# Window attention with a Sinkhorn mixture of experts: the products of two Strassen groups in one interleaved order, and the first unit's weight work placed later

## The chip, the cores and the metric

The kernel runs on one core of one Trainium2 chip. The metric is the device time of one execution in microseconds (us); before the change it is 1629.33 us, the median of three runs (1628.76 to 1629.43). The engines are TensorE (PE; its weight loads are listed apart as PEld), VectorE (DVE), ScalarE (ACT), GpSimd (POOL) and SyncE (SP), whose queue issues the DMAs. Each engine takes its instructions in the order in which they were written.

## The reference, cut to what matters

Attention in a window of 64 positions, then a soft mixture of eight experts, whose weights come from a Sinkhorn iteration. Everything is float32. The experts' two matrix products take most of the time:

```python
def _moe_ref(x, w_gate, w1, w2):          # x: 2304 x 512, w1: 8 x 512 x 1024, w2: 8 x 1024 x 512
    logits = x @ w_gate
    logits = logits - logits.max()
    P = np.exp(logits)
    for _ in range(8):
        P /= P.sum(1, keepdims=True) + 1e-09
        P /= P.sum(0, keepdims=True) + 1e-09
        P *= N / E
    for e in range(E):
        h = np.maximum(x @ w1[e], 0.0)
        ye = h @ w2[e]
        out += P[:, e:e + 1] * ye
```

## The kernel before

A first phase (up to about 207 us) computes the attention and part of the first expert for all rows. The second phase is what the change touches. It goes over the rows in three passes of six tiles of 128 rows; the inputs x of a pass lie in SBUF as sums and differences (`xc`, seven of them). Each expert's 1024 hidden columns are taken 256 at a time; one such piece is a **group** (90 in all), and two groups make a **unit** (45 units, 15 in each pass).

**A group's first product** is done with Strassen's scheme in Winograd's form: seven products of 2 x 2 blocks, numbered 1 to 7, instead of eight. Each product is six matmuls of 384 columns (`product`, line 175): the float32 operands are split into a high and a low part in fp32r, and high x high, high x low and low x high are added. Products add up in three PSUM banks: 1 and 2 in bank a (profile name `qa`), 6, 7 and 4 in b (`qb`), 5 and 3 in c (`qc`). Each bank exists twice and a group takes one of each, so two groups can be open at once. Between the products other engines read the banks:

- ScalarE copies bank a after product 1 to `p1` (line 195; the profile calls it `p`).
- VectorE (`add`, line 188) adds bank b after product 6 to `p1`, giving `u2`; bank b after product 7 to `p1`, giving `u3`; bank c after product 5 to `u3`; bank b after product 4 to `p1`; bank c after product 3 to `u2`. The profile calls `u2` and `u3` both `u`.
- ScalarE (`relu`, line 180) makes the high part of the four quarters of the hidden activations `g`, from bank a after product 2, from `u3`, from `p1` and from `u2`. VectorE (`low`, line 185) makes the low parts of the same four. The first of the four reads a PSUM bank and an SBUF tile, the other three read two SBUF tiles.

A product may write a bank again only when what was read from it before has been read: product 2 waits for the copy, products 7 and 4 for the adds of bank b, and product 3 for the add that reads bank c after product 5.

**A unit** is: the seven products of its even group, the seven of its odd group, then 72 matmuls of 512 columns (`mm2`, line 235), which multiply the activations of both groups by `w2` and whose sums VectorE adds to the output tiles (`acc`).

**The weights of later groups** are prepared along the way. `fetch1` and `fetch2` issue the loads of w1 and w2 of a group into a ring of three buffers (`stg`) on the SyncE queue; a load waits until the buffer's last content has been used. `sums1` forms four sums of w1's blocks on GpSimd (lines 126 to 129). `split1` and `split2` make high parts on ScalarE (lines 143, 155) and low parts on GpSimd (lines 146, 156). In unit u with groups s and s+1, the code before calls: during the even group `split2(s+2)` and `fetch1(s+3)`, during the odd group `sums1(s+2)`, `split2(s+3)` and `fetch2(s+4)`, after the products `split1(s+2)`, `sums1(s+3)` and `fetch2(s+5)`, and after the third tile of `mm2` `split1(s+3)` and `fetch1(s+4)`. Ahead of the first unit stand, in this order, `fetch2(1)`, `split1(1)`, `split2(0)`, `split2(1)`, `fetch2(2)`, `fetch2(3)`, `fetch1(2)`; behind them comes the start of the Sinkhorn iteration, whose exponential is on ScalarE (line 674).

The order of everything is the order of the code: no scheduler moves an instruction.

Of the kernel before, what the change touches and what calls it, by code (L numbers as in the profile page):

```python
# [21 lines left out]
def window_attention_sinkhorn_moe(ctx: ExitStack, tc: tile.TileContext, q, k, v, w_gate, w1, w2, out):  # L22
    nc = tc.nc
# [51 lines left out]
    class Ring:  # L75
# [5 lines left out]
        def open(self, pool):  # L81
            if self.nb:
                self.pool_b, self.n, self.i = pool, self.na + self.nb, self.na
# [21 lines left out]
    def fetch1(i):  # L105
        if i < len(groups):
            _, e, c = groups[i]
            stg = r_stg.new()
            nc.sync.dma_start(out=stg, in_=w1[e, :, c * 2 * P:(c + 1) * 2 * P].rearrange("(k p) f -> p k f", p=P))
            raw1[i] = stg  # L110

    def fetch2(i):
        if i < len(groups):
            _, e, c = groups[i]
            stg = r_stg.new().rearrange("p k f -> p (k f)").rearrange("p (c d) -> p c d", c=2)
            nc.sync.dma_start(out=stg, in_=w2[e, c * 2 * P:(c + 1) * 2 * P, :].rearrange("(c p) d -> p c d", p=P))
            raw2[i] = stg
# [31 lines left out]
    def split2(i):  # L149
        if i >= len(groups):  # L150
            return
        src = raw2.pop(i)
        for j in range(2):
            w = r_w2.new()
            nc.scalar.copy(out=w[:, 0], in_=src[:, j])  # L155
            nc.gpsimd.tensor_tensor(out=w[:, 1], in0=src[:, j], in1=f32(w[:, 0]), op=ALU.subtract)  # L156
            wt2[i, j] = w
# [4 lines left out]
    ps = {}  # L162
    gt_ = {}

    class Group:
# [21 lines left out]
        def add(self, dst, bank, src):  # L187
            nc.vector.tensor_tensor(out=dst, in0=bank, in1=src, op=ALU.add)  # L188

        def run(self, extra):  # L190

            a, b, c = ps["a"](), ps["b"](), ps["c"]()
            p1, u2, u3 = r_p.new(), r_u2.new(), r_u3.new()
            self.product(1, a, True)
            nc.scalar.copy(out=p1, in_=a)  # L195
            extra(0)
            self.product(6, b, True)
            self.add(u2, b, p1)
            self.product(2, a, False)
            self.relu(0, 0, a)  # L200
            extra(1)
            self.product(7, b, False)
            self.add(u3, b, p1)
            self.low(0, 0, a)
            self.product(5, c, True)
            self.add(u3, c, u3)
            self.relu(1, 1, u3)
            self.product(4, b, False)
            self.add(p1, b, p1)
            self.relu(1, 0, p1)  # L210
            self.low(1, 1, u3)
            extra(2)
            self.product(3, c, False)
            self.add(u2, c, u2)
            self.relu(0, 1, u2)
            self.low(1, 0, p1)
            self.low(0, 1, u2)
            extra(3)
            wt1.pop(self.i)


    side = {}
# [64 lines left out]
    with tc.manual_schedule():  # L287
# [348 lines left out]
        with ExitStack() as p2:  # L636
            ring_b = p2.enter_context(tc.tile_pool(name="ring_b", bufs=1, reuse_waits="tile"))
            sk_p = p2.enter_context(tc.tile_pool(name="sk", bufs=2, reuse_waits="tile"))
            ps_m = p2.enter_context(tc.tile_pool(name="ps_m", bufs=2, space=PSUM, reuse_waits="tile"))
            for nm in "abc":  # L640
                ps[nm] = lambda nm=nm: ps_m.tile([P, 512], F32, tag=f"q{nm}", name=f"q{nm}")[:, :NB]
            ps["y"] = lambda: ps_m.tile([P, 512], F32, tag="y", name="yp2")
            for r in rings.values():
                r.open(ring_b)

            def side_tile():
                return ring_b.tile([P, 4 * 2 * NB], F32, tag="side", name="side")

            side["acc"] = side_tile().rearrange("p (t d) -> p t d", t=TP)
            fetch2(1)  # L650
            split1(1)
            split2(0)
            split2(1)
            fetch2(2)
            fetch2(3)
            fetch1(2)


            pending = []
            state = {}  # L660

            def sk_tile(shape, name):
                n = 1
                for x in shape[1:]:
                    n *= x
                t = ps["c"]()[:shape[0], :n]
                return t.rearrange("p (t e) -> p t e", e=shape[2]) if len(shape) == 3 else t

            def sk_exp():
                mp = sk_tile([P, 1], "mb")  # L670
                nc.tensor.matmul(mp, lhsT=ones[0:1, :], rhs=max2, start=True, stop=True)
                nm = sk_p.tile([P, 1], F32, tag="nm", name="nm2", bufs=1)
                nc.vector.tensor_copy(out=nm, in_=mp)
                nc.scalar.activation(out=pv, in_=logit, func=AF.Exp, bias=nm)

            def sk_row():
                r = sk_p.tile([P, T], F32, tag="r", name="r")
                nc.vector.tensor_reduce(out=r, in_=prob[:, 0:T, :], axis=AX.X, op=ALU.add)
                nc.vector.reciprocal(out=r, in_=r)
                nc.vector.tensor_tensor(out=pv, in0=pv, in1=r[:, :, None].to_broadcast([P, T, E]), op=ALU.mult)  # L680

            def sk_col():
                cp = sk_tile([P, T + 1, E + 1], "cp")
                nc.tensor.matmul(cp, lhsT=part, rhs=prob, start=True, stop=True)
                c = sk_p.tile([P, E], F32, tag="c", name="c")
                nc.vector.tensor_reduce(out=c, in_=cp[:, :, 0:E].rearrange("p t e -> p e t"), axis=AX.X, op=ALU.add)
                nc.vector.reciprocal(out=c, in_=c)
                nc.vector.tensor_tensor(out=pv, in0=pv, in1=c[:, None, :].to_broadcast([P, T, E]), op=ALU.mult)

            sk_exp()  # L690
            sk_row()
            pending += [lambda: (sk_col(), sk_row())] * (ITERS - 1) + [sk_col]

            def step():
                if pending:
                    pending.pop(0)()


            def next_sums(p, j):
                if j == 0:  # L700
                    side["xt"] = side_tile().rearrange("p (i k n) -> p i k n", i=4, k=2)
                x = ring_b.tile([P, KD, 2 * P], F32, tag="xr2", name="xr2")
                nc.sync.dma_start(out=x, in_=xd_f[p - 1][j])
                x_sums(side["xt"][:, :, :, j * P:(j + 1) * P], x, nc.gpsimd)

            def next_slot(p, slot):
                if slot < 3:
                    nc.sync.dma_start(out=f32(xc[slot]), in_=xd_r[p - 1][:, slot])
                else:
                    nc.scalar.copy(out=xc[slot][:, 0], in_=side["xt"][:, slot - 3])  # L710

            def next_low(slot):
                nc.vector.tensor_tensor(out=xc[slot][:, 1], in0=side["xt"][:, slot - 3], in1=f32(xc[slot][:, 0]), op=ALU.subtract)

            n_units = len(groups) // 2
            per = n_units // NPASS
            for u in range(n_units):
                pas, at = divmod(u, per)
                more = pas + 1 < NPASS
                s = 2 * u  # L720

                edge = more and at == per - 1

                def even(k):
                    if k == 1:
                        split2(s + 2)
                        fetch1(s + 3)
                    elif k == 3 and more and per - 5 <= at < per - 5 + TP // 2:
                        next_sums(pas + 1, at - (per - 5))

                def odd(k):
                    if k == 0:
                        sums1(s + 2)
                    elif k == 1:
                        split2(s + 3)
                        fetch2(s + 4)
                    if edge and k in (0, 1, 3):
                        next_slot(pas + 1, (0, 1, None, 2)[k])

                Group(s).run(even)  # L740
                Group(s + 1).run(odd)
                order = (4, 5, 3, 6)
                if edge:
                    for slot in order:
                        next_slot(pas + 1, slot)
                split1(s + 2)
                sums1(s + 3)
                fetch2(s + 5)
                for t in range(TP):
                    mm2(u, t)  # L750
                    if t % 2 == 0:
                        step()
                    if t == 2:
                        split1(s + 3)
                        fetch1(s + 4)
                    if edge and t < 4:
                        next_low(order[t])
# [28 lines left out]
```

## Time and profile before

| | us |
|---|---|
| median of three runs | 1629.33 |
| the profiled execution | 1628.85 |
| its span, first to last instruction | 1626.8 |
| TensorE busy in it | 1608.7 |
| GpSimd busy | 1010.4 |
| VectorE busy | 828.4 |
| ScalarE busy | 623.1 |

The rows come from one profiled execution. Times in a timeline are microseconds from the start of its span. A timeline row gives start, length, engine, line, operation, output and inputs; "x6" is six instructions in one row, whose length goes from the first one's start to the last one's end. Matmuls are pipelined, so that rows of neighbouring products overlap by some 0.16 us; where a product's turn begins is read from the starts. In brackets stands how long the engine was idle ahead of the row and which instruction ended that.

### The profile page before, as it was taken

How to read it: one execution, taken by the hardware profiler on the slowest of the kernel's cores; microseconds unless marked ns; L12 is line 12 of the kernel's file. 1: busy time of each engine (PE TensorE's matmuls, PEld its weight loads, DVE VectorE, ACT ScalarE, POOL GpSimd, SP SyncE). 2: the span in 40 equal slices, each digit the busy share in tenths (PEclk: the TensorE clock that was granted, in tenths of full speed). 3: DMA queues.
4: the chain of work that ended last, by engine and by line, in shares of the span. 5: the costliest groups of instructions: out<-in, count | busy, mean ns of one | idle time of the engine just before them, and what ended most of it. 6: DMA issues, size and time to landing. Idle time of an engine off the chain costs nothing.

```text
span 1626.8 us, 23899 instructions
## 1 busy us (share of the span) xinstructions
PE 1608.7 (99%) x9253; PEld 1432.6 (88%) x9253; DVE 828.4 (51%) x1411; ACT 623.1 (38%) x1267; POOL 1010.4 (62%) x942
## 2 busy tenths in 40 slices
PE   8999989999999999999999999999999999999999
PEld 6888879988988998998898899899889889989988
DVE  6666455664544454554454445445545445544543
ACT  5666533342342333334333233333433323423331
POOL 5244475676666668676666656876756666675670
PEclk9999999999999999999999999999999999999999
DMA  9876531222222222432122212222622222221211
GB/s 216 195 166 147 152 117 52 65 78 65 65 66 77 65 91 78 152 114 78 65 65 71 73 54 77 91 78 85 194 65 65 78 65 64 66 75 56 67 50 39
DMA packets 156624, 145.86 MB, mean 90 GB/s; under 512 B 62112, under 2 KB 123040, under 8 KB 156512
## 3 DMA queue, kind: packets, MB, share of 16 engines
q1 hardware_dynamic: 156512, 144.35, 30.2%
q8 instruction: 72, 1.18, 0.3%
q14 instruction: 40, 0.33, 0.1%
HBM read 121.65 MB, written 15.73 MB: 84 GB/s over the span
## 4 chain that ended last, share of the span: by engine, by line
PE 96%; DVE 1%; DMA 1%; ACT 1%; issue 0%; SPq 0%; POOL 0%; ACTq 0%; POOLq 0%; DVEq 0%
PE yp L235 45%; PE qb L175 17%; PE qa L175 12%; PE qc L175 12%; PE yp L519 3%; PE hp L505 3%; PE vp L425 1%; PE sp L375 1%; PE tp L410 1%; PE tp L347 1%; DMA q<-in_q_dram 1%; ACT s L394 0%; DMA stg<-in_moe_w_dram 0%; DVE nm L382 0%; DVE s L379 0%
## 5 line engine op out<-in xcount | busy, mean ns | idle before, releaser
L235 PE MATMUL yp<-w2c,g 128*128 128x512 f32 x3240 | 746.6, 390 | 0.0
L235 PEld LDWEIGHTS yp<-w2c,g 128*128 128x128 f32 x3240 | 607.0, 188 | 125.0 <-DVE acc L255 0.9
L156 POOL TENSOR_TENSOR w2c<-stg,w2c 128x512 fp32r<-128x512 f32 x180 | 229.1, 1295 | 326.3 <-PE qb L175 315.1
L255 DVE SCALAR_TENSOR_TENSOR acc<-yp,prob,acc 128x512 f32<-128x512 f32 x240 | 180.2, 751 | 412.6 <-PE yp L235 405.7
L175 PE MATMUL qb<-xc,w1c 128*128 128x384 f32 x1620 | 328.6, 337 | 0.0
L175 PEld LDWEIGHTS qb<-xc,w1c 128*128 128x128 f32 x1620 | 284.1, 188 | 4.0 <-DVE u L188 0.6
L146 POOL TENSOR_TENSOR w1c<-stg,w1c 128x512 fp32r<-128x512 f32 (+1 forms) x180 | 179.7, 1020 | 103.8 <-ACT w1c L143 103.8
L175 PE MATMUL qa<-xc,w1c 128*128 128x384 f32 x1080 | 223.0, 341 | 5.5 <-ACT p L195 5.0
L146 POOL TENSOR_TENSOR w1c<-ws,w1c 128x1024 fp32r<-128x1024 f32 x90 | 218.4, 2426 | 0.0
L175 PE MATMUL qc<-xc,w1c 128*128 128x384 f32 x1080 | 216.4, 335 | 0.0
L175 PEld LDWEIGHTS qa<-xc,w1c 128*128 128x128 f32 x1080 | 189.7, 189 | 19.0 <-ACT p L195 15.0
L188 DVE TENSOR_TENSOR u<-qb,p 128x384 f32<-128x384 f32 x180 | 99.9, 555 | 199.0 <-PE qb L175 198.8
L143 ACT CAST w1c<-ws 128x1024 fp32r<-128x1024 f32 x90 | 94.7, 1052 | 252.7 <-POOL ws L129 252.7
L175 PEld LDWEIGHTS qc<-xc,w1c 128*128 128x128 f32 x1080 | 190.5, 188 | 0.0
L180 ACT ACTIVATE g<-u 128x384 fp32r<-128x384 f32 x180 | 94.7, 526 | 173.9 <-DVE u L188 172.2
L195 ACT COPY p<-qa 128x384 f32<-128x384 f32 x90 | 42.6, 473 | 272.6 <-PE qa L175 272.6
L185 DVE SCALAR_TENSOR_TENSOR g<-u,g 128x384 fp32r<-128x384 f32 x180 | 139.6, 775 | 8.0
L155 ACT CAST w2c<-stg 128x512 fp32r<-128x512 f32 x180 | 101.9, 617 | 8.6 <-DMA stg<-in_moe_w_dram 8.6
L188 DVE TENSOR_TENSOR u<-qc,u 128x384 f32<-128x384 f32 x180 | 99.9, 555 | 2.6
L180 ACT ACTIVATE g<-qa 128x384 fp32r<-128x384 f32 x90 | 44.2, 491 | 135.6 <-PE qa L175 135.6
L404 POOL TENSOR_TENSOR s<-s,rr 128x512 f32<-128x512 f32 x36 | 37.5, 1040 | 78.1 <-DVE rr L403 41.2
L143 ACT CAST w1c<-stg 128x512 fp32r<-128x512 f32 (+1 forms) x180 | 82.4, 506 | 5.0 <-DMA stg<-in_moe_w_dram 5.0
(124 smaller groups left out, 1324.4 us busy)
## 6 DMA issues: line engine op xcount, KB each, us to landing
stg<-in_moe_w_dram SPq DMA_DIRECT2D x182, 512.0 KB, 3.5
xd_r<-xs SPq DMA_DIRECT2D x36, 128.0 KB, 2.6
xc<-xd_r SPq DMA_DIRECT2D x6, 768.0 KB, 5.8
out_dram<-acc SPq DMA_DIRECT2D x18, 256.0 KB, 3.1
vs<-v SPq DMA_DIRECT2D x35, 128.0 KB, 4.1
k<-in_k_dram SPq DMA_DIRECT2D x16, 256.0 KB, 4.7
q<-in_q_dram SPq DMA_DIRECT2D x16, 256.0 KB, 5.2
v<-in_v_dram SPq DMA_DIRECT2D x16, 256.0 KB, 4.1
```

The costliest lines, as they stand in the source:

```text
L143: nc.scalar.copy(out=w[:, 0, sl].rearrange("p s k f -> p (s k) f"), in_=src)
L146: nc.gpsimd.tensor_tensor(out=o, in0=src, in1=f32(h), op=ALU.subtract)
L155: nc.scalar.copy(out=w[:, 0], in_=src[:, j])
L156: nc.gpsimd.tensor_tensor(out=w[:, 1], in0=src[:, j], in1=f32(w[:, 0]), op=ALU.subtract)
L175: nc.tensor.matmul(bank, lhsT=w[:, a, ws, kk, :], rhs=xc[xs][:, b, kk, :], start=(first and j == 0), stop=(j == 5), skip_group_check=not f ...
L180: nc.scalar.activation(out=g[:, 0, :], in_=src, func=AF.Relu)
L185: nc.vector.scalar_tensor_tensor(out=g[:, 1, :], in0=src, scalar=0.0, in1=f32(g[:, 0, :]), op0=ALU.max, op1=ALU.subtract)
L188: nc.vector.tensor_tensor(out=dst, in0=bank, in1=src, op=ALU.add)
L235: nc.tensor.matmul(yp, lhsT=g[:, a, o:o + P], rhs=w[:, x, :], start=(i == 0), stop=(i == 11))
L255: nc.vector.scalar_tensor_tensor(out=at, in0=yp, scalar=pr, in1=at, op0=ALU.mult, op1=ALU.add)
L505: nc.tensor.matmul(hp, lhsT=w1s[c][:, a, kk, :], rhs=xs[j][:, b, kk, :], start=(i == 0), stop=(i == 3 * KD - 1))
L519: nc.tensor.matmul(yp, lhsT=g[:, a, o * P:(o + 1) * P], rhs=w[:, x, :], start=(i == 0), stop=(i == 11))
```

## The change

The method `run` of a group becomes nine short methods, and a unit calls those of its two groups (g, the even one, and h, the odd one) in an order written out. The seven products of a group stay as they are. Their order in a unit was g1 g6 g2 g7 g5 g4 g3, then the same of h; it becomes g1 g6 g5 g2 g7 h1 g4 h6 g3 h2 h7 h5 h4 h3. The reads of the banks on VectorE and ScalarE go with the products, except that g's read of c for `u3` follows h's copy, and that g's last low part (`end`) follows h7. `split2(s+2)` moves to just ahead of g2, `sums1(s+2)` to behind h1, and `split2(s+3)` to behind h2.

The second part concerns the first unit alone. `split2(1)` and `fetch1(2)` move from ahead of it to behind h2, and `split2(2)`, `fetch1(3)`, `sums1(2)`, `split2(3)` and `fetch2(4)` from its products to behind them.

```diff
-        def run(self, extra):
...
+        def open(self):
+            self.p1, self.u2, self.u3 = r_p.new(), r_u2.new(), r_u3.new()
+            self.a = ps["a"]()
+            self.product(1, self.a, True)
+            nc.scalar.copy(out=self.p1, in_=self.a)
+
+        def b6(self):
+            self.b = ps["b"]()
+            self.product(6, self.b, True)
+            self.add(self.u2, self.b, self.p1)
+
+        def a2(self):
+            self.product(2, self.a, False)
+            self.relu(0, 0, self.a)
+
+        def b7(self):
+            self.product(7, self.b, False)
+            self.add(self.u3, self.b, self.p1)
+
+        def c5(self):
+            self.c = ps["c"]()
+            self.product(5, self.c, True)
+
+        def c22(self):
+            self.low(0, 0, self.a)
+            self.add(self.u3, self.c, self.u3)
+            self.relu(1, 1, self.u3)
+
+        def b4(self):
+            self.product(4, self.b, False)
+            self.add(self.p1, self.b, self.p1)
+            self.relu(1, 0, self.p1)
+            self.low(1, 1, self.u3)
+
+        def c3(self):
+            self.product(3, self.c, False)
+            self.add(self.u2, self.c, self.u2)
+            self.relu(0, 1, self.u2)
+            self.low(1, 0, self.p1)
             wt1.pop(self.i)
+
+        def end(self):
+            self.low(0, 1, self.u2)
...
             split2(0)
-            split2(1)
             fetch2(2)
             fetch2(3)
-            fetch1(2)
...
                 def even(k):
+                    if u == 0:
+                        return
...
                 def odd(k):
-                    if k == 0:
+                    if u == 0:
+                        if k == 1:
+                            split2(1)
+                            fetch1(2)
+                    elif k == 0:
                         sums1(s + 2)
...
-                Group(s).run(even)
-                Group(s + 1).run(odd)
+                g, h = Group(s), Group(s + 1)
+                g.open()
+                even(0)
+                g.b6()
+                g.c5()
+                even(1)
+                g.a2()
+                g.b7()
+                h.open()
+                odd(0)
+                g.c22()
+                g.b4()
+                even(2)
+                h.b6()
+                g.c3()
+                h.a2()
+                odd(1)
+                even(3)
+                h.b7()
+                g.end()
+                h.c5()
+                h.c22()
+                h.b4()
+                odd(2)
+                h.c3()
+                h.end()
+                odd(3)
...
-                split1(s + 2)
+                if u == 0:
+                    split2(2)
+                    fetch1(3)
+                    sums1(2)
+                    split1(2)
+                    split2(3)
+                    fetch2(4)
+                else:
+                    split1(s + 2)
                 sums1(s + 3)
                 fetch2(s + 5)
```

What that makes of the order of the instructions is shown at three places. The rows are those of unit 21, whose timeline is among the rows below; the other units after the first have the same. A number behind a name tells instances apart, and `w1c_0`, `p1_0`, `u2_0`, `u3_0` belong to g, `w1c_1`, `p1_1`, `u2_1`, `u3_1` to h; `xc0` to `xc6` are the seven inputs, one for each product (0 for product 1, 1 for 2, 2 for 3, 6 for 4, 3 for 5, 4 for 6, 5 for 7).

TensorE, the seven products of h in the unit before:

```order
L175 MATMUL qa_8858<-xc0_81,w1c_1_8733 128x384 x6
L175 MATMUL qb_8859<-xc4_85,w1c_1_8733 128x384 x6
L175 MATMUL qa_8858<-xc1_82,w1c_1_8733 128x384 x6
L175 MATMUL qb_8859<-xc5_86,w1c_1_8733 128x384 x6
L175 MATMUL qc_8860<-xc3_84,w1c_1_8733 128x384 x6
L175 MATMUL qb_8859<-xc6_87,w1c_1_8733 128x384 x6
L175 MATMUL qc_8860<-xc2_83,w1c_1_8733 128x384 x6
```

TensorE, the same unit after, from g's third product on:

```order
L175 MATMUL qc_8803<-xc3_84,w1c_0_8677 128x384 x6
L175 MATMUL qa_8787<-xc1_82,w1c_0_8677 128x384 x6
L175 MATMUL qb_8795<-xc5_86,w1c_0_8677 128x384 x6
L175 MATMUL qa_8836<-xc0_81,w1c_1_8733 128x384 x6
L175 MATMUL qb_8795<-xc6_87,w1c_0_8677 128x384 x6
L175 MATMUL qb_8863<-xc4_85,w1c_1_8733 128x384 x6
L175 MATMUL qc_8803<-xc2_83,w1c_0_8677 128x384 x6
L175 MATMUL qa_8836<-xc1_82,w1c_1_8733 128x384 x6
L175 MATMUL qb_8863<-xc5_86,w1c_1_8733 128x384 x6
L175 MATMUL qc_8905<-xc3_84,w1c_1_8733 128x384 x6
L175 MATMUL qb_8863<-xc6_87,w1c_1_8733 128x384 x6
L175 MATMUL qc_8905<-xc2_83,w1c_1_8733 128x384 x6
```

Three products stand between h's products on `xc0` and `xc1` (1 and 2), where there was one; between the last two on `qc` stands one product, as before.

VectorE at the end of g and the start of h's tail, before:

```order
L185 SCALAR_TENSOR_TENSOR g0_5_8844<-p1_0_8787,g0_5_8844 128x384
L185 SCALAR_TENSOR_TENSOR g1_1_8854<-u2_0_8788,g1_1_8854 128x384
L188 TENSOR_TENSOR u2_1_8862<-qb_8859,p1_1_8861 128x384
L188 TENSOR_TENSOR u3_1_8863<-qb_8859,p1_1_8861 128x384
L185 SCALAR_TENSOR_TENSOR g0_0_8889<-qa_8858,g0_0_8889 128x384
L188 TENSOR_TENSOR u3_1_8863<-qc_8860,u3_1_8863 128x384
L188 TENSOR_TENSOR p1_1_8861<-qb_8859,p1_1_8861 128x384
```

VectorE after, in the stretch in which h's products 7, 5 and 4 are read:

```order
L185 SCALAR_TENSOR_TENSOR g0_5_8860<-p1_0_8784,g0_5_8860 128x384
L188 TENSOR_TENSOR u3_1_8835<-qb_8863,p1_1_8833 128x384
L185 SCALAR_TENSOR_TENSOR g1_1_8878<-u2_0_8785,g1_1_8878 128x384
L185 SCALAR_TENSOR_TENSOR g0_0_8887<-qa_8836,g0_0_8887 128x384
L188 TENSOR_TENSOR u3_1_8835<-qc_8905,u3_1_8835 128x384
L188 TENSOR_TENSOR p1_1_8833<-qb_8863,p1_1_8833 128x384
```

The low part of g's `u2` now stands between h's adds of `qb` and of `qc` for `u3`, ahead of the low part from `qa`.

ScalarE at the start of the first unit, before (the first two rows are the casts of `split2(1)`):

```order
L155 CAST w2c_6_3167<-stg_2_3152 128x512
L155 CAST w2c_7_3170<-stg_2_3152 128x512
L674 ACTIVATE prob_74<-logit_73,nm2_3181 128x18x8
L195 COPY p1_0_3191<-qa_3188 128x384
L180 ACTIVATE g0_4_3214<-qa_3188 128x384
L155 CAST w2c_0_3216<-stg_0_3173 128x512
L155 CAST w2c_1_3219<-stg_0_3173 128x512
```

ScalarE after:

```order
L685 ACTIVATE prob_74<-logit_73,nm2_3173 128x18x8
L194 COPY p1_0_3180<-qa_3183 128x384
L180 ACTIVATE g0_4_3212<-qa_3183 128x384
L194 COPY p1_1_3221<-qa_3224 128x384
L180 ACTIVATE g1_0_3234<-u3_0_3182 128x384
L180 ACTIVATE g0_5_3243<-p1_0_3180 128x384
L180 ACTIVATE g1_1_3261<-u2_0_3181 128x384
L180 ACTIVATE g0_0_3270<-qa_3224 128x384
L155 CAST w2c_6_3272<-stg_2_3152 128x512
L155 CAST w2c_7_3275<-stg_2_3152 128x512
```

The exponential and g's copy no longer have casts ahead of them; the casts of `split2(1)` stand behind h's first Relu.

## Rows read from the trace of the kernel before

**Rows 1.** The page: the span, the busy time of TensorE, and of its costliest groups the weight loads for bank c (line, engine, operation, output and inputs, count, busy us, mean ns of one, then idle us ahead of them).

```profile
span 1626.8 us, 23899 instructions
PE 1608.7 (99%) x9253; PEld 1432.6 (88%) x9253; DVE 828.4 (51%) x1411; ACT 623.1 (38%) x1267; POOL 1010.4 (62%) x942
...
L175 PEld LDWEIGHTS qc<-xc,w1c 128*128 128x128 f32 x1080 | 190.5, 188 | 0.0
```

**Rows 2.** The waits of TensorE's weight loads from 246 us to the end: who waited for whom, us in total, times, longest.

```profile
PEld qa L175 <- ACT p L195: 9.6, 36, 0.3
...
PEld qb L175 <- DVE u L188: 0.3, 1, 0.3
```

**Rows 3.** The timeline of TensorE's matmuls in unit 21 (873.76 to 905.02 us): product 5 and 3 of g, product 2 of h.

```profile
877.98 1.20 PE L175 MATMUL qc<-xc,w1c 128*128 128x384 f32 x6
...
880.06 1.20 PE L175 MATMUL qc<-xc,w1c 128*128 128x384 f32 x6
...
883.29 1.31 PE L175 MATMUL qa<-xc,w1c 128*128 128x384 f32 x6
```

**Rows 4.** The timeline of the weight loads in the same unit: of product 3 of g, 6 and 2 of h, and 3 of h.

```profile
879.88 1.05 PEld L175 LDWEIGHTS qc<-xc,w1c 128*128 128x128 f32 x6
...
881.97 1.05 PEld L175 LDWEIGHTS qb<-xc,w1c 128*128 128x128 f32 x6
883.29 0.99 PEld L175 LDWEIGHTS qa<-xc,w1c 128*128 128x128 f32 x6 [0.27 <-ACT p L195]
...
887.45 1.05 PEld L175 LDWEIGHTS qc<-xc,w1c 128*128 128x128 f32 x6
```

**Rows 5.** The timelines of ScalarE, VectorE and GpSimd in the same unit.

```profile
877.10 0.49 ACT L180 ACTIVATE g<-qa 128x384 fp32r<-128x384 f32 x1 [1.55 <-PE qa L175]
...
882.34 0.53 ACT L180 ACTIVATE g<-u 128x384 fp32r<-128x384 f32 x1 [0.97 <-DVE u L188]
882.77 0.46 ACT L195 COPY p<-qa 128x384 f32<-128x384 f32 x1
...
878.17 0.56 DVE L188 TENSOR_TENSOR u<-qb,p 128x384 f32<-128x384 f32 x1 [1.49 <-PE qb L175]
878.65 0.55 DVE L185 SCALAR_TENSOR_TENSOR g<-qa,g 128x384 fp32r<-128x384 f32 x1
879.21 0.56 DVE L188 TENSOR_TENSOR u<-qc,u 128x384 f32<-128x384 f32 x1
...
880.73 1.11 DVE L185 SCALAR_TENSOR_TENSOR g<-u,g 128x384 fp32r<-128x384 f32 x1
881.77 0.54 DVE L188 TENSOR_TENSOR u<-qc,u 128x384 f32<-128x384 f32 x1
...
885.73 0.56 DVE L188 TENSOR_TENSOR u<-qb,p 128x384 f32<-128x384 f32 x1 [1.40 <-PE qb L175]
...
878.18 1.30 POOL L156 TENSOR_TENSOR w2c<-stg,w2c 128x512 fp32r<-128x512 f32 x1 [7.20 <-PE qb L175]
...
880.69 0.74 POOL L126 TENSOR_TENSOR ws<-stg 128x256 f32<-128x256 f32 x1
...
885.71 1.30 POOL L156 TENSOR_TENSOR w2c<-stg,w2c 128x512 fp32r<-128x512 f32 x1 [1.26 <-PE qb L175]
```

**Rows 6.** All instances of line 185 by their inputs: count, then shortest, median and longest in ns.

```profile
L185 DVE SCALAR_TENSOR_TENSOR g<-u,g x180: 547/560/1134, 221.8 to 1607.8; 128x384 fp32r<-128x384 f32 x180
L185 DVE SCALAR_TENSOR_TENSOR g<-qa,g x90: 547/548/549, 219.7 to 1604.0; 128x384 fp32r<-128x384 f32 x90
```

**Rows 7.** The timelines of VectorE and GpSimd in the first unit, where line 680 (the Sinkhorn iteration's division of a row, two SBUF inputs) meets line 156.

```profile
215.28 1.21 DVE L680 TENSOR_TENSOR prob<-prob,r 128x144 f32<-128x144 f32 x1
...
215.06 1.27 POOL L156 TENSOR_TENSOR w2c<-stg,w2c 128x512 fp32r<-128x512 f32 x1
```

**Rows 8.** The timelines of TensorE and ScalarE in the first unit: products 1, 2 and 5 of g, the first matmuls of `mm2`, the casts of `split2(1)` and the copy.

```profile
207.62 1.33 PE L175 MATMUL qa<-xc,w1c 128*128 128x384 f32 x6 [0.48 <-DVE nm L673]
...
215.00 2.29 PE L175 MATMUL qa<-xc,w1c 128*128 128x384 f32 x6 [5.01 <-ACT p L195]
...
219.02 1.21 PE L175 MATMUL qc<-xc,w1c 128*128 128x384 f32 x6
...
229.42 2.92 PE L235 MATMUL yp<-w2c,g 128*128 128x512 f32 x12
...
213.13 1.14 ACT L155 CAST w2c<-stg 128x512 fp32r<-128x512 f32 x2 [8.61 <-DMA stg<-in_moe_w_dram]
...
214.49 0.46 ACT L195 COPY p<-qa 128x384 f32<-128x384 f32 x1
```

**Rows 9.** Busy time by stretch: the stretch, its length, busy us (and instructions) of PE, PEld, DVE, ACT and POOL, TensorE's granted clock as a share of full speed, the share of the DMA engines and GB/s.

```profile
215.00:217.00 2.00, 2.00 (x6) 1.78 (x6) 1.93 (x3) 0.00 (x0) 1.33 (x2) 0.50 0.03 11
...
15.00:20.00 5.00, 3.39 (x55) 2.71 (x52) 3.19 (x9) 4.31 (x14) 2.61 (x3) 0.75 0.97 203
25.00:30.00 5.00, 3.04 (x58) 2.55 (x59) 3.63 (x7) 4.19 (x9) 4.00 (x5) 1.00 0.83 138
873.76:905.02 31.26, 31.26 (x158) 28.04 (x156) 14.86 (x24) 10.69 (x20) 20.27 (x18) 1.00 0.22 68
```

**Rows 10.** The timeline of TensorE in unit 12, in which no wait stands: its first product and the first matmuls of `mm2`.

```profile
592.83 1.23 PE L175 MATMUL qa<-xc,w1c 128*128 128x384 f32 x6
...
607.48 0.63 PE L235 MATMUL yp<-w2c,g 128*128 128x512 f32 x2
```

More of the change, by code (lines that the diff above doesn't have):

```diff
@@ L188, in add @@
             nc.vector.tensor_tensor(out=dst, in0=bank, in1=src, op=ALU.add)
-        def run(self, extra):
[L192 to L218, printed above, removed]
+        def open(self):
[30 more added lines that the diff above has]
+            self.low(1, 0, self.p1)
             wt1.pop(self.i)
+        def end(self):
+            self.low(0, 1, self.u2)
     side = {}
```

## The prediction

> **What bounds the kernel now.** Three views, in this order. The page says how much can be won at all: TensorE is busy for 99% of a span of 1626.8 us [rows 1], so nothing counts but its waits and whatever slows its matmuls. The waits by releaser then name the wait that comes back in every unit: after the first unit TensorE's weight load for bank qa waited 9.6 us in 36 places for the ScalarE copy p of line 195, 0.27 us each [rows 2]. The timeline of one unit in the middle, engine by engine, shows why, and it is also the view on which the new order can be laid. I call the two groups of a unit g and h.
>
> In that unit g's low part of u3 (line 185, both inputs in SBUF) started at 880.73 and took 1.11 us, where the fastest take 0.55 [rows 5, 6]. GpSimd had begun its sum of line 126 at 880.69 for 0.74 us, to 881.43, and the low part ended 0.41 us after that, at 881.84 [rows 5]. Low parts that read a PSUM bank (g<-qa) never took over 0.549 us in 90 instances [rows 6], also beside GpSimd (878.65, with line 156 running from 878.18 [rows 5]). So a VectorE operation with both inputs in SBUF waits here until the running GpSimd instruction has ended. The first unit shows it for the very instruction that matters below: line 156 ran from 215.06 for 1.27 us, to 216.33; VectorE's line 680 (both inputs in SBUF) started at 215.28 and ended at 216.49 [rows 7]. The late low part pushes VectorE's add to 881.77, ScalarE's Relu to 882.34 and its copy of h's p1 to 882.77 to 883.23. TensorE loads for h's product 2 at 883.29, and its turn was 881.97 + 1.05 = 883.02 [rows 3, 4, 5]: the 0.27 us. What counts is the load's time, since loads run ahead of the matmuls (879.88 against 880.06 for product 3 [rows 3, 4]), and a wait costs from there.
>
> **The old wait goes: -9.6.** New order: g1 g6 g5 g2 g7 h1 g4 h6 g3 h2 h7 h5 h4 h3. Between products 1 and 2 of a group now stand two or three products of 1.04 us instead of one, and ScalarE copies h's p1 right behind h1, ahead of g's last Relus. A copy of 0.46 us has over 2 us, so all 36 waits go and nothing else is due there. The GpSimd sums (lines 126 to 129) move ahead by some two products; VectorE's SBUF-only work lies behind them then, so they cost nothing.
>
> **The first unit: -7.15.** ScalarE reached the casts of w2 for group 1 (line 155) before their data and stood idle 8.61 us, to 213.13; the copy p1 behind them came at 214.49, and TensorE waited 5.01 us, to 215.00 [rows 8]. After it the granted clock was 0.50 of 215 to 217 (the 1.2 GHz level) [rows 9], and the two products from 215.00 to 219.02 took 4.02 us instead of 2.08. All 14 products took 229.42 - 207.62 = 21.80 us [rows 8]; in a unit without any wait 607.48 - 592.83 = 14.65 [rows 10]. The casts now follow the tenth product, at about 218, five us after their data, and the copy follows its product. What could be late next are the weights of groups 2 and 3, prepared from about 219 on instead of in the products. GpSimd works 20.3 us in a whole unit [rows 9]; begun at 219.4, with some 5 us for the two loads that now wait for a buffer, it is through at about 245. Unit 1 starts at about 241 with group 2 (some 10 us of that work), and group 3's first product comes five products later, at 246. So it costs 0; if that cover fails, 0 to 2 us.
>
> **The new wait: +49.5.** Look at the end of a unit. Products h5, h4, h3 are on qc, qb, qc: between the two on qc stands one. Product h3 may only write qc when VectorE's add has read it for u3. VectorE's queue there was add(qb), low(qa), add(qc); it is now add(qb), low(u2 of g), low(qa), add(qc). The rows give the price for that queue, since h2, h7, h5, h4, h3 still run back to back as g2, g7, g5, g4, g3 do. Before: add(qb) at 878.17, low(qa) 878.65, add(qc) 879.21 to 879.77. TensorE saw it some 0.06 us later (copy end 883.23, load 883.29), at 879.83, and its load was due at 879.88 [rows 4, 5]. The margin is 0.05 us. One more low part takes 0.56 us from start to start (878.65 to 879.21), so a wait of 0.51 us is sure if the add binds at all.
>
> And that low part has both inputs in SBUF and meets GpSimd. Line 156 of split2(s+3) starts 1.08 us after the Relu of h's qa (877.10, 878.18 [rows 5]), which h keeps: Relu and casts still follow h2. So GpSimd's 1.30 us begin with VectorE's add(qb) (878.18 and 878.17; in h 885.71 and 885.73) and the low part arrives 0.48 us later, in their middle. It ends at 878.18 + 1.30 + 0.41 = 879.89. The next operation starts 0.07 us ahead of that record (881.77 against 881.84): low(qa) 879.82, add(qc) 880.38 to 880.94, seen at 881.00, against 879.88: 1.12 us. From h's rows (885.71, load due at 887.45 [rows 4, 5]) the same walk gives 1.08. I take 1.10, in all 45 units, the first too: 45 x 1.10 = 49.5. The other banks keep the 0.05 us margin that they had (one wait of 0.3 us on qb in all units [rows 2]): 0.
>
> The Trainium skill ("SBUF — State Buffer", section "SBUF: two separate sides") has the shared port pair of VectorE and GpSimd as an exclusive lock: who starts first keeps it for the whole instruction, and the other "fully blocks". The waiting is what rows 5 and 7 show; the trace disagrees with a full block, since the low part ended 0.41 us after GpSimd and not its whole 0.55. By the page the sum would be some 6 us more (45 x 0.14), an estimate.
>
> **The sum.** 1626.8 - 9.6 - 7.15 + 49.5 = 1659.6 us of span. The profiled execution took 1628.85, 2.05 more than its span; that makes 1661.6. The median of the three runs, 1629.33, is 0.48 above it: 1662.1. So some 2% slower.
>
> **Rivals.** (1) GpSimd comes late. If something holds the Relu of h's qa by over 0.48 us, the low part is first, and the wait is 0.51: 45 x 0.51 = 23.0, and 1610.05 + 23.0 + 2.5 = 1635.6. Against it: on ScalarE g's last Relu stands ahead and ends about when h2 does; it would have to slip by half a product. For it: sums that wait for their load can slow VectorE before it. Chance 0.09.
>
> (2) Not slower: the add does not decide product h3. The place is h3's first matmul; the price is 0 instead of 1.10, from the point where the add is seen by 879.88 on the scale of that unit, or TensorE's wait names an earlier VectorE operation. Then only the gains stay: 1626.8 - 16.75 + 2.5 = 1612.6. For it: in all 180 groups of before qc's loads never waited (idle 0.0 [rows 1]), so no row proves that this edge can stop TensorE. Against it: the add reads the bank that h3 writes, 879.83 against 879.88 fits a wait that never came to light, and the same edge on qb did stop it once. Chance 0.08. A half of it, the low part first and only the matmul's own start (880.06, 0.18 later than its load) counting, is 0.33 x 45 = 14.9 us, or 1627.5: 0.03.
>
> (3) The clock falls at each new wait. Two products lost 1.94 us after the idle time of 5 us [rows 8, 9]; 45 x 1.94 = 87 more makes 1749. Rows of the first phase stand on both sides: in 15 to 20 us, TensorE busy 3.39 of 5, the clock was 0.75, in 25 to 30, busy 3.04 of 5, it was 1.00 [rows 9]. One gap of 1.1 us in 32 busy ones is far from either. The Trainium skill ("TensorE: Matmul & The Clock Gate", section "A second HAM failure mode: psum-queue depth-cycling") tells of short idle times between groups of matmuls that made the clock swing in one kernel; the 36 waits of 0.27 here did not (1.00 in 873.76 to 905.02 [rows 9]). Chance 0.05.
>
> That the products stay in their old order is no rival: the rows of the change show them moved.
>
> **How the numbers follow.** The forecast has 0.75, the rivals 0.09, 0.08, 0.03 and 0.05. About 0.2% (3.3 us) is what a measurement here can tell from no change. Slower by more: 0.75 + 0.09 + 0.05 = 0.89; faster: 0.08; within: 0.03. The forecast alone goes from 1652 (a wait of 0.9) to 1670 (the page's 6 us and 2 us for the first unit). With 0.75 it does not hold 8 in 10, so the range reaches down to rival (1): 1634 to 1670 holds 0.84.
>
> **What would show it.** Right: in TensorE's waits, qc's weight load waits for VectorE's add of line 188 some 45 times, about 1.1 us each; qa's waits for the copy are gone; the low part of g's u2 shows 1.2 us beside line 156; a middle unit takes 32.1 us and the first one's products 15.7. Wrong: qc's loads without idle time (rival 2), a low part of 0.55 there (rival 1), or a granted clock under 1.00 after the first unit (rival 3).

## The result, and the profile after

| | before | after |
|---|---|---|
| median, us | 1629.19 (4 runs) | 1652.68 (4 runs) |
| span of the profiled execution, us | 1626.8 | 1650.9 |

The ratio is 1.0144, with a 95% interval of 1.0126 to 1.0161: the change makes the kernel 1.4% slower. 1662 was forecast, in a range of 1634 to 1670.

The waits of TensorE's weight loads from 246 us to the end, as in [rows 2]:

```profile
PEld qc L175 <- DVE u L188: 43.5, 44, 1.0
PEld yp L248 <- DVE acc L268: 0.8, 3, 0.4
```

The waits for ScalarE's copy are gone, and one on bank c stands in each unit, where the loads for qc never waited before [rows 1]. All but one of the 44 are 1.00 or 1.01 us long; the last unit, below, has 0.28. A unit in the middle shows it: TensorE's first product and the next unit's; the loads of h's products 4 and 3; VectorE from the read of h's product 7 on; GpSimd.

```profile
881.20 1.23 PE L175 MATMUL qa<-xc,w1c 128*128 128x384 f32 x6
...
913.10 1.23 PE L175 MATMUL qa<-xc,w1c 128*128 128x384 f32 x6
...
893.53 1.05 PEld L175 LDWEIGHTS qb<-xc,w1c 128*128 128x128 f32 x6
895.59 0.99 PEld L175 LDWEIGHTS qc<-xc,w1c 128*128 128x128 f32 x6 [1.01 <-DVE u L188]
...
892.86 0.56 DVE L188 TENSOR_TENSOR u<-qb,p 128x384 f32<-128x384 f32 x1 [1.06 <-PE qb L175]
893.34 1.27 DVE L185 SCALAR_TENSOR_TENSOR g<-u,g 128x384 fp32r<-128x384 f32 x1
894.53 0.54 DVE L185 SCALAR_TENSOR_TENSOR g<-qa,g 128x384 fp32r<-128x384 f32 x1
895.00 0.54 DVE L188 TENSOR_TENSOR u<-qc,u 128x384 f32<-128x384 f32 x1
...
892.90 1.30 POOL L156 TENSOR_TENSOR w2c<-stg,w2c 128x512 fp32r<-128x512 f32 x1 [3.86 <-PE qb L175]
```

Read it from below. GpSimd's line 156 begins at 892.90, 0.04 us behind VectorE's read of qb, and runs to 894.20. The low part of g's u2 comes at 893.34, into its middle, and ends at 894.61, 0.41 us after GpSimd. Only then come the low part of qa and the add that reads qc, to 895.54; h3's load follows at 895.59, when 893.53 + 1.05 = 894.58 was its turn. The unit lasts 31.90 us, 0.64 more than the one of [rows 9].

The last unit has no later groups whose weights must be prepared, so GpSimd is idle in it. VectorE's low part of g's u2, and TensorE's load of h3:

```profile
1627.41 0.55 DVE L185 SCALAR_TENSOR_TENSOR g<-u,g 128x384 fp32r<-128x384 f32 x1
...
1628.94 1.00 PEld L175 LDWEIGHTS qc<-xc,w1c 128*128 128x128 f32 x6 [0.28 <-DVE u L188]
```

The same low part takes 0.55 us there instead of 1.27, and the load waits 0.28 instead of 1.01.

The first unit (TensorE: products 1 of g and 3 of h, first matmuls of `mm2`), as in [rows 8]:

```profile
207.62 1.31 PE L175 MATMUL qa<-xc,w1c 128*128 128x384 f32 x6 [0.48 <-DVE nm L684]
...
222.16 1.33 PE L175 MATMUL qc<-xc,w1c 128*128 128x384 f32 x6 [0.74 <-DVE u L188]
223.32 2.92 PE L248 MATMUL yp<-w2c,g 128*128 128x512 f32 x12
```

Its products take 15.70 us instead of 21.80, with one new wait in them. The granted clock of the rest is 1.00:

```profile
240.70:1650.00 1409.30, 1376.42 (x6875) 1235.73 (x6873) 660.32 (x1093) 485.34 (x903) 876.77 (x802) 1.00 0.23 76
```

### The profile page after: what moved, and what is told of

The parts are those of the page before. It is cut to its first block, busy times and chain, and to the rows that moved or that the text cites. A ratio compares the mean times of both kernels' runs of the same rounds, so it can differ in the third digit from the quotient of the medians.

```text
span 1650.9 us, 23824 instructions
## 1 busy us (share of the span) xinstructions
PE 1608.2 (97%) x9253; PEld 1431.6 (87%) x9253; DVE 809.0 (49%) x1411; ACT 620.8 (38%) x1267; POOL 987.1 (60%) x942
## 4 chain that ended last, share of the span: by engine, by line
PE 89%; DVE 6%; issue 3%; ACT 1%; POOL 0%; ACTq 0%; DVEq 0%; POOLq 0%
PE yp L248 45%; PE qb L175 14%; PE qa L175 11%; PE qc L175 9%; PE yp L532 3%; DVE u L188 3%; PE hp L518 2%; DVE g L185 2%; PE vp L438 1%; PE tp L423 1%; PE sp L388 1%; PE tp L360 1%; ACT s L407 0%; DVE xs L445 0%; DVE nm L395 0%
## 5 line engine op out<-in xcount | busy, mean ns | idle before, releaser
L156 POOL TENSOR_TENSOR w2c<-stg,w2c 128x512 fp32r<-128x512 f32 x180 | 241.9, 1365 | 348.7 <-ACT w2c L155 189.0
L175 PE MATMUL qb<-xc,w1c 128*128 128x384 f32 x1620 | 317.1, 334 | 0.0
L175 PE MATMUL qc<-xc,w1c 128*128 128x384 f32 x1080 | 221.4, 339 | 30.2 <-DVE u L188 30.2
L175 PEld LDWEIGHTS qc<-xc,w1c 128*128 128x128 f32 x1080 | 187.1, 188 | 44.6 <-DVE u L188 44.6
L175 PE MATMUL qa<-xc,w1c 128*128 128x384 f32 x1080 | 217.4, 335 | 0.5 <-DVE nm L684 0.5
L185 DVE SCALAR_TENSOR_TENSOR g<-u,g 128x384 fp32r<-128x384 f32 x180 | 132.2, 734 | 11.3
L126 POOL TENSOR_TENSOR ws<-stg 128x256 f32<-128x256 f32 x90 | 68.1, 756 | 11.3 <-DMA stg<-in_moe_w_dram 8.0
```

The lines of the kernel that those rows point to most:

```text
L126: nc.gpsimd.tensor_tensor(out=ws[:, 0], in0=a21, in1=a22, op=ALU.add)
L175: nc.tensor.matmul(bank, lhsT=w[:, a, ws, kk, :], rhs=xc[xs][:, b, kk, :], start=(first and j == 0), stop=(j == 5), skip_group_check=not f ...
L185: nc.vector.scalar_tensor_tensor(out=g[:, 1, :], in0=src, scalar=0.0, in1=f32(g[:, 0, :]), op0=ALU.max, op1=ALU.subtract)
```

## Experiments

Theory: product h3 waits for VectorE's queue, which the low part of g's u2 lengthens, and GpSimd's line 156 makes that low part more than twice as long. Rivals: it waits because only one product stands between the two on bank c; it waits by the queue's length alone; the first unit's part gives nothing.

### The low part behind the add

```diff
                 h.b7()
-                g.end()
                 h.c5()
                 h.c22()
+                g.end()
```

> One line of the changed kernel is moved: the low part of g's u2 (end) goes from between h7's and h5's reads to behind h's add of bank c, so that VectorE's queue there is add(qb), low(qa), add(qc) as before the change; the products keep their order. Theory (VectorE's queue ahead of product h3, lengthened by that low part): in the changed kernel's timeline the add of qc would then end at 1.48 us after the start of add(qb) and be seen at 1.53, and the load of h3 is due at 1.72, so qc's load waits go from 43.5 us to about 0 and the unit from 31.91 to about 30.94; 1652.7 - 45 x 0.97 = 1609, 1606 to 1613. Rival (the wait comes from there being only one product between the two on qc): nothing of that is changed, qc's loads wait about 1.0 us in every unit and the time stays at 1650 to 1655.

Measured: 1610.39 us, ratio 0.9888 (0.9873 to 0.9903) to the kernel before. TensorE's loads and VectorE's queue at the same place:

```profile
873.55 1.05 PEld L175 LDWEIGHTS qb<-xc,w1c 128*128 128x128 f32 x6
874.59 1.05 PEld L175 LDWEIGHTS qc<-xc,w1c 128*128 128x128 f32 x6
...
872.88 0.56 DVE L188 TENSOR_TENSOR u<-qb,p 128x384 f32<-128x384 f32 x1 [1.06 <-PE qb L175]
873.36 0.55 DVE L185 SCALAR_TENSOR_TENSOR g<-qa,g 128x384 fp32r<-128x384 f32 x1
873.92 0.56 DVE L188 TENSOR_TENSOR u<-qc,u 128x384 f32<-128x384 f32 x1
874.40 1.49 DVE L185 SCALAR_TENSOR_TENSOR g<-u,g 128x384 fp32r<-128x384 f32 x1
```

The add ends at 874.48, 1.60 us after the start of add(qb) and not 1.48, since it still waits for product 5; the load for qc takes its turn all the same. The products stand as in the change, with one between the two on bank c, so the distance on the bank alone is not what makes h3 wait. The low part now takes 1.49 us beside GpSimd, and nobody waits for it. One moved line takes 42 us off, and the kernel is 1.1% faster than before the change.

### GpSimd's line 156 later

```diff
                 h.a2()
-                odd(1)
                 even(3)
...
                 h.c22()
+                odd(1)
```

> The changed kernel with split2(s+3) (casts, line 156, and the load behind it) moved from behind h2 to behind h's reads for u3, so that GpSimd is idle when the low part of g's u2 runs; the low part stays where it is. Theory (the length of the queue plus GpSimd's lock): the low part takes 0.55 instead of 1.27 us, the add of qc is seen about 0.35 us after h3's load is due, and the time is 1609 + 45 x 0.33 = 1624, 1620 to 1629. Rival (the queue alone, the lock is hidden or no cause): qc's wait stays at about 1.0 us and the time at 1650 to 1655. Second rival (the wait of h3 is all lock): 1609.

Measured: 1623.01 us, ratio 0.9966 (0.9953 to 0.9979). The low part, line 156 and the load of h3:

```profile
879.27 0.56 DVE L188 TENSOR_TENSOR u<-qb,p 128x384 f32<-128x384 f32 x1 [1.06 <-PE qb L175]
879.74 0.55 DVE L185 SCALAR_TENSOR_TENSOR g<-u,g 128x384 fp32r<-128x384 f32 x1
...
882.37 2.87 POOL L156 TENSOR_TENSOR w2c<-stg,w2c 128x512 fp32r<-128x512 f32 x2 [6.93 <-ACT w2c L155]
...
881.28 0.99 PEld L175 LDWEIGHTS qc<-xc,w1c 128*128 128x128 f32 x6 [0.28 <-DVE u L188]
```

With GpSimd out of the way the same low part takes 0.55 us, and the wait is 0.28 instead of 1.01. So 0.73 us of the wait are GpSimd's and 0.28 the queue's.

### Two neighbours exchanged

```diff
                 h.b7()
-                g.end()
                 h.c5()
+                h.low(0, 0, h.a)
+                g.end()
                 h.c22()
```

(`c22` no longer makes that low part for h; the line added does.)

> The changed kernel with two neighbouring VectorE instructions exchanged: the low part of h's qa stands ahead of the low part of g's u2. Same instructions, same number ahead of the add of qc. Theory (lock): line 156 holds until 1.34 us after the start of add(qb) as before, the low part of u2 still ends at about 1.75, but only the add stands behind it, 0.47 us less: h3's load waits 0.5 to 0.55 instead of 1.01 and the time is 1609 + 45 x 0.5 = 1631, 1627 to 1636. Rival (only the number of instructions ahead of the add counts): no change, 1650 to 1655.

Measured: 1632.18 us, ratio 1.0021 (1.0012 to 1.0030).

```profile
883.49 0.55 DVE L185 SCALAR_TENSOR_TENSOR g<-qa,g 128x384 fp32r<-128x384 f32 x1
883.96 0.80 DVE L185 SCALAR_TENSOR_TENSOR g<-u,g 128x384 fp32r<-128x384 f32 x1
884.68 0.55 DVE L188 TENSOR_TENSOR u<-qc,u 128x384 f32<-128x384 f32 x1
...
883.05 2.85 POOL L156 TENSOR_TENSOR w2c<-stg,w2c 128x512 fp32r<-128x512 f32 x2 [3.86 <-PE qb L175]
...
885.28 1.00 PEld L175 LDWEIGHTS qc<-xc,w1c 128*128 128x128 f32 x6 [0.54 <-DVE u L188]
```

The same instructions in another order halve the wait. The low part that reads a PSUM bank runs while GpSimd works, and the one with both inputs in SBUF waits only for what is left of line 156 (0.80 instead of 1.27 us). So the count of instructions ahead of the add does not decide alone.

### The new order without the first unit's part

The lines of the diff on `u == 0`, `split2(1)` and `fetch1(2)` are undone.

> The changed order of the products in all units, with the weight work of the first unit where it stood before the change. Theory: the first unit waits again for the copy behind casts whose data are not there: three products instead of two run ahead of it, so 4.1 us of waiting instead of 5.0 and up to 2 us at the 1.2 GHz level; 1652.7 + 4.1 to 6.1 = 1656.8 to 1658.8. Rival (the first unit's part gives nothing, its gain is lost to weights that come late): 1652.7.

Measured: 1659.58 us, ratio 1.0189 (1.0172 to 1.0206), 0.8 above the upper end of what was expected. TensorE's products g2, g7 and h1, VectorE's read of product 6, and a stretch with its granted clock:

```profile
214.78 1.32 PE L175 MATMUL qa<-xc,w1c 128*128 128x384 f32 x6 [3.87 <-ACT p L194]
216.81 2.29 PE L175 MATMUL qb<-xc,w1c 128*128 128x384 f32 x6 [0.70 <-DVE u L188]
218.90 2.12 PE L175 MATMUL qa<-xc,w1c 128*128 128x384 f32 x6
...
215.05 1.23 DVE L693 TENSOR_TENSOR prob<-prob,r 128x144 f32<-128x144 f32 x1
216.21 0.54 DVE L188 TENSOR_TENSOR u<-qb,p 128x384 f32<-128x384 f32 x1
...
217.00:219.00 2.00, 2.00 (x7) 2.00 (x8) 0.00 (x0) 0.00 (x0) 1.65 (x2) 0.50 0.79 251
```

The wait for the copy and the 1.2 GHz level are there as expected. What was not expected is the second wait: g7 needs the read of product 6, which stands behind the Sinkhorn division. That came late with the exponential, and beside GpSimd's line 156 it took 1.23 us, where it takes 0.53 in the changed kernel.

### The first unit's part alone

The old order with the lines of the diff on `u == 0`, `split2(1)` and `fetch1(2)`.

> The kernel before with the first unit's part of the change alone; the products keep their old order. Theory: ScalarE's copy no longer stands behind casts that wait for data, the first unit loses its wait of 5.0 us and the 1.94 us at the 1.2 GHz level: 1629.2 - 7.15 = 1622.0, 1620.5 to 1624. Rival (the weights of groups 2 and 3, now prepared later, are missing in unit 1): 1624 to 1629, with waits of TensorE's loads for GpSimd's line 146 about 235 to 250 us.

Measured: 1620.89 us, ratio 0.9953 (0.9939 to 0.9966). Its first unit's products (first product and first matmuls of `mm2`):

```profile
207.46 1.31 PE L175 MATMUL qa<-xc,w1c 128*128 128x384 f32 x6 [0.47 <-DVE ys L525]
...
222.16 2.92 PE L235 MATMUL yp<-w2c,g 128*128 128x512 f32 x12
```

14.70 us instead of 21.80, and no load waits for line 146 afterwards. This half of the change gains what the forecast gave it.

### The old wait without the new order

```diff
                 def odd(k):
-                    if k == 0:
-                        sums1(s + 2)
-                    elif k == 1:
+                    if k == 1:
                         split2(s + 3)
                         fetch2(s + 4)
+                        sums1(s + 2)
```

> The kernel before with one call moved: sums1(s+2) goes from behind h1 to behind split2(s+3), so that GpSimd is idle when VectorE makes g's low parts; products in their old order, first unit as before. Theory (the old wait comes from GpSimd's sums holding up VectorE's low parts, as the new one comes from line 156): the low parts of g's u3 take 0.55 instead of 1.11 us, ScalarE's copy is in time, the 36 waits of 0.27 us for it go: 1629.2 - 9.4 = 1619.8, 1618.5 to 1621.5. Rival (the old wait comes from the Relus that stand ahead of the copy on ScalarE, and needs the interleaved order to go away): 1627 to 1630.

Measured: 1622.98 us, ratio 0.9964 (0.9952 to 0.9977): 5.9 us, not 9.4, and outside the expected range. Its waits from 246 us on:

```profile
PEld yp L235 <- DVE acc L255: 3.6, 5, 1.6
PEld qb L175 <- DVE u L188: 0.3, 1, 0.3
PEld qa L175 <- ACT p L195: 0.2, 1, 0.2
```

All but one of the 36 waits for the copy are gone, as by the theory. The size was missed. Loads wait 3.6 us in all for the output tiles, in units 3, 16 and 31 (the first unit is 0), where it was 0.9 before. In these units ScalarE scales the output tiles (line 252). Its queue in unit 16, and the VectorE row that waits for it:

```profile
734.48 1.05 ACT L143 CAST w1c<-ws 128x1024 fp32r<-128x1024 f32 x1 [0.82 <-POOL ws L129]
735.43 1.94 ACT L252 ACTIVATE acc<-acc,prob 128x512 f32<-128x512 f32 x3
...
736.18 1.41 DVE L255 SCALAR_TENSOR_TENSOR acc<-yp,prob,acc 128x512 f32<-128x512 f32 x2 [2.33 <-ACT acc L252]
```

The scaling stands behind casts of w1 that now wait 0.82 us for the moved sums (line 129), so VectorE comes to the output tiles late. Another 0.7 us are lost in the first unit, where the granted clock was still 0.66 from 219.0 to 220.5 us, against 1.00 before.

### Both gains in the old order, and the best version again

The first unit's part, and `sums1` late from unit 4 on, except in a pass's last unit.

> The old order of the products, with the first unit's part of the change, and with sums1(s+2) behind split2(s+3) from unit 4 on except in the last unit of a pass (where the moved sums had met VectorE's work on the output tiles). Theory (both gains of the change come from weight work that is placed better, not from the interleaved products): units of 31.01 us without a wait, all but some six, 1628.9 - 8.0 - 8.5 = 1612.4, 1611 to 1614. Against the version with the interleaved order and no wait (1610.4): the interleaved units are 30.95 and not 31.01 us long, 45 x 0.06 = 2.7, and that is all the new order is worth. Rival (the interleaved order is needed for the gain): 1620 or more.

> The version with the low part of g's u2 behind the add of bank c a second time, on the same chip as the version with the old order, so that the two can be set side by side: 1610.4 against 1612.4 by the theory above, 1620 or more for the other by the rival.

Measured on one chip: 1614.65 us, ratio 0.9912 (0.9895 to 0.9928), and 1610.43, ratio 0.9887 (0.9872 to 0.9902). The old order reaches all but 4.2 us of the best version, where about 2 were expected, and lies 0.65 above the expected range. What it still waits for the output tiles, the copies and the adds, from 200 us on, and what the best version does (last line):

```profile
PEld yp L235 <- DVE acc L255: 2.3, 5, 0.7
PEld qa L175 <- ACT p L195: 1.3, 5, 0.3
...
PEld qb L175 <- DVE u L188: 0.3, 1, 0.3
...
PEld yp L248 <- DVE acc L268: 1.6, 3, 0.9
```

The five waits for the copy stand in units 1, 2, 3, 14 and 29, which are just those where the sums kept their old place: in the old order it is moving the sums that takes the old wait away. The waits for the output tiles stand in units 3, 16 and 31 again. Units 16 and 31 are the second ones of their passes, so the exception for the last unit of a pass missed them. Of the 4.2 us, some 2.3 are these waits (3.9 against 1.6), and some 2 are units that are 0.05 us longer in the old order (below).

So most of the gain does not need the interleaved products: 14.0 of 18.2 us come without them.

## Why the prediction was right

**The old wait, -9.6: right,** and so was its cause. Moving the sums alone takes away all but one of the 36 waits in the old order. In the changed kernel the copy also ends 2.27 us ahead of the load (887.66 + 0.48 = 888.14 against 890.41), as the prediction had it ("over 2 us"); no run separates the copy's earlier place there from that of the sums.

**The first unit, -7.15: right.** Alone it gave 7.10 in that stretch (21.80 to 14.70), with 8.0 us between the medians. Its cover held, by 0.6 us: GpSimd's low parts of w1 for group 3 ended at 245.12, the load of that group's first product began at 245.74, and no load waited for the later weights.

**The new wait, +49.5: right in place and mechanism, too large.** The step that was mis-sized is "One more low part takes 0.56 us from start to start (878.65 to 879.21)", used also for the low part of qa ahead of the add. In that row the add was waiting for TensorE's product 5, which ended just ahead of it (877.98 + 1.20 = 879.18 [rows 3]). VectorE's own distance is 0.47 us (894.53 to 895.00). The load waits 1.01 us instead of 1.10, and the unit is 0.97 longer than in the version without the wait (31.92 and 30.95, means of 38 units from unit 4 or 5 on): 45 x 0.968 = 43.6. For the same reason the wait without GpSimd is 0.28 and not 0.51.

**What the sum left out, -3.0:** units without any wait last 30.95 us in the new order and 31.00 in the old one (nine in a row of the kernel with late sums), 45 x 0.05. And the last unit, without line 156, waits 0.28 and not 1.01: -0.7. 1662.1 - 5.9 - 2.3 - 0.7 = 1653.2; measured 1652.7. In the run with late sums the longer time stands at products 7 and 5 of each group (875.22 to 877.33 and 882.53 to 884.62, 2.11 and 2.09 us, where two products take 2.08); why stays open.

**The rivals.** Rival (1) did not happen: GpSimd began 0.04 us after the read of qb. Its own price, by the run with line 156 later, was 1623 and not 1635.6, so it would have been a gain, though the prediction counted its chance as slower. Rival (2) fell: the add does decide h3, and in the old order it had 0.05 us to spare, which no wait could show. (The "180 groups" of that rival are the 180 products on bank c of 90 groups; only the 90 products 3 write behind an add.) Rival (3) fell: 43 waits of 1.0 us left the granted clock at 1.00. The Trainium skill's case of short idle times between groups of matmuls ("TensorE: Matmul & The Clock Gate", section "A second HAM failure mode: psum-queue depth-cycling") does not appear in this trace.

The prediction read the full block of the Trainium skill ("SBUF — State Buffer", section "SBUF: two separate sides") as the whole 0.55 us still to come. That was the worse figure again: the low part ended 0.41 us after GpSimd (894.20, 894.61). But the whole 0.55 was the prediction's own step, and "the trace disagrees with a full block" says too much. What is left when GpSimd ends grows with the columns: 0.16 us for 144 [rows 7], 0.41 for 384, and 0.55 for 512, as these rows of VectorE and GpSimd before the change show:

```profile
331.20 2.04 DVE L254 SCALAR_TENSOR_TENSOR acc<-side,prob,acc 128x512 f32<-128x512 f32 x1
...
329.79 2.90 POOL L146 TENSOR_TENSOR w1c<-ws,w1c 128x1024 fp32r<-128x1024 f32 x1
```

That is about 1.1 ns a column in all three (an estimate from these rows). It fits an operation whose work on the columns all waits, and of which only some fixed part runs beside GpSimd; no run tests that reading.

## What to carry to other kernels

Where one engine is busy all the time, a new order of its work is judged by the queues of the others: write down what stands between a bank's release and its next use, one engine at a time, and against how much slack. Here a VectorE operation with two SBUF inputs that started beside a running GpSimd instruction ended only after it, by 0.41 us for 384 columns; put it behind whatever the bound engine waits for, and put operations that read PSUM ahead. A start-to-start time read from a trace can hide a wait; check that the input was there long before.

## What the runs showed of the hardware

- The order of two neighbouring VectorE operations, one on PSUM and one on SBUF alone, was worth 0.47 us a unit beside a GpSimd instruction (waits of 1.01 and 0.54).
- A VectorE operation with two SBUF inputs that met a running GpSimd instruction ended 0.16 us after it with 144 columns, 0.41 with 384 and 0.55 with 512.
- Idle times of 3.9 us (new order without the first unit's part) and 5.0 us [rows 8] were followed by a granted clock of 0.50; single waits of 1.0 us, once in 32 us, were not (1.00 from 240.70 us to 1650).
